# Strassen products for the last pair and the first two single tiles, a re-measured plan, and a new order of the first loads, in a fused attention and MLP kernel

## The chip, the cores and the metric

The kernel runs on one core of a Trainium2 chip. The metric is the device time of one execution in microseconds (us). Most executions of one kernel lie within 0.3% of each other. The span in a profile is some 1.8 us shorter than the device time of the same execution, because it counts from the first instruction to the last. A run over 1.5% above the fastest of the same kernel is called slow, and no reading here rests on a slow run.

## The reference, cut to what matters

Eight-head attention over 4 batches of 768 positions with a band of 96 positions and 8 global columns, then a two-layer MLP on the 3072 x 512 result.

```python
B, H, S, D = 4, 8, 768, 64
keep = is_global | is_local            # 8 global columns, band of 96
scores = np.where(keep, scale * q @ k.T + bias, -1e9)
x = softmax(scores) @ v                # gathered to 3072 x 512
h = x @ w_in                           # 512 x 2048
g = h - np.tanh(h)
out = g @ w_out                        # 2048 x 512
```

The sequence is cut into 24 tiles of 128 rows. The first four tiles go through the MLP singly, the other twenty in ten pairs.

## The kernel before

TensorE (PE) does scores, attention times v, transposes, and the two products of the MLP. The second product, g with w_out, has two forms. The plain one takes 16 matmuls of 512 columns for each tile. The other is Strassen's scheme on a pair of tiles: rows are halved by tile, the 2048 inner positions by halves, and the 512 columns by halves, so that seven products of 8 matmuls of 256 columns stand for the eight block products of the plain form (56 x 256 columns of work against 64 x 256, which the plain form does as 32 x 512). VectorE (DVE) makes the sums of g that go in (A), the sums of w_out (B, made once), and the sums that make the output out of the seven products.

```python
FAST = set(range(5, 13))         # groups done by Strassen: eight of the ten pairs
ORDER = (4, 3, 1, 5, 2, 7, 6)    # the seven products
HOME = {3: ("in", 0), 4: ("in", 1), 1: ("one", 0), 5: ("mid", 0), 2: ("mid", 1),
        7: ("out", 0), 6: ("out", 1)}          # which PSUM bank, which half of it
...
def product(g, kk):                            # 8 matmuls of 256 columns
    n, side = HOME[kk]
    o = buf("bank", ("P", g, n))[:, side * DH : side * DH + DH]
    for f in range(CH):
        ...
        nc.tensor.matmul(o, a, b, start=(f == 0), stop=(f == CH - 1))
```

Products 7 and 6, the last two, share one PSUM bank. The last group of all is not done by Strassen: its last tile is computed in 384 and 128 columns, so that only a copy and a small store follow the last matmul.

No instruction stands in program order by hand. A planner in the kernel file holds every operation with its engine, a duration, what it comes after and which buffers it takes and gives; it simulates the engines and the loads, and the kernel is emitted in the order of the simulated starts. Loads of q, k and v are given to the queue of GpSimd (POOL) in a list, and from tile 6 on each waits until the first product of the MLP has come near enough to its tile.

```python
LAT = {PE: 0.2, ACT: 0.14, DVE: 0.13, POOL: 0.15, SP: 0.0}   # end to release
...
AHEAD, EARLIER = 5.0, 0.5        # how many tiles ahead of its use a tile's work begins
MORE = 0.0
arrive = "q0 v2 v0 q1 k1 v1 q2 k2 i0 i1 q3 i2 i3 k3 i4 i5 o0 v3 k0 o1 k4 q5 o2 v6 o3 q4 k5 q6 k6 v4 v5".split()
...                              # i0.. parts of w_in, o0.. parts of w_out
hw_loads = {0}                   # q and k of tile 0: as float over the SP queue, cast on chip
...
pl.op(("g", g, f), DVE, 0.66, lambda e, g=g, f=f: m1_g(g, f), after=[("th", g, f)], ...)
```

The softmax here doesn't subtract the row's maximum and nothing guards it: scores larger than these inputs give would overflow.

Of the kernel before, what the change touches and what calls it, by code (L numbers as in the profile page):

```python
# [16 lines left out]
class Planner:  # L17


    LAT = {PE: 0.2, ACT: 0.14, DVE: 0.13, POOL: 0.15, SP: 0.0}  # L20
# [17 lines left out]
    def run(self, free, prefer):  # L38
# [5 lines left out]
        rings = {SP: [], POOL: []}  # L44
        setup, finish = {SP: 1.1, POOL: 2.0}, {SP: 0.3, POOL: 0.5}
# [17 lines left out]
        def step(limit):  # L63
            nonlocal at_dma
            heads = {r: x[0] for r, x in rings.items() if x}
            live = [r for r, x in heads.items() if x[2] <= at_dma + 1e-9]
            if not heads:
                at_dma = max(at_dma, limit) if limit < never else at_dma
                return None
            nxt = min([x[2] for r, x in heads.items() if r not in live] + [limit])  # L70
            hw = 0.07 if len(live) == 2 and heads[POOL][3] else 0.41
            rate = {r: (hw if r is SP else 1.0 - hw) if len(live) == 2 else 1.0 for r in live}
            end = min([at_dma + heads[r][1] / rate[r] for r in live] + [never])
            t = min(nxt, end)
            for r in live:
                heads[r][1] -= (t - at_dma) * rate[r]
            at_dma = t
            for r in live:
                if heads[r][1] < 1e-9:
                    return r  # L80
            return None
# [17 lines left out]
        while left:  # L99
# [36 lines left out]
            if o["dma"]:  # L136
                rings[eng].append([key, o["dma"], end + setup[eng], key[0] in ("in", "out")])
# [29 lines left out]
def kernel(  # L167
# [31 lines left out]
    TILES = [(0, 0), (1, 0), (0, 1), (0, 2), (1, 1), (2, 0), (0, 3), (2, 1), (3, 0), (3, 1), (1, 2), (2, 2), (1, 3), (3, 2), (0, 4), (2, 3), (3, 3), (3, 4), (0, 5), (1, 4), (1, 5), (3, 5), (2, 4), (2, 5)]  # L199
# [4 lines left out]
    R_ENGS = [(ACT, 0.7), (DVE, 0.36)]  # L204
    FAST = set(range(5, 13))
# [22 lines left out]
    touch = [cpool.tile([P, CD, 16], FP32, name=f"touch{n}") for n in range(2)]  # L228
# [6 lines left out]
    IN_PARTS = [2, 2, 2, 2, 4, 4]  # L235
# [6 lines left out]
    sb("kf", [P, H, Dh], FP32, 2)  # L242
# [21 lines left out]
    sb("ot", [P, DM], FP32, 3)  # L264
    sb("ot2", [P, 2, DM], FP32, 2)
# [11 lines left out]

    def fast(g):
        return g in FAST

    def gtags(g):
        return [("g", g)] if len(groups[g]) > 1 else [("g", g, 0), ("g", g, 1)]
# [4 lines left out]
    def gblk(g, f0, f1, c0, c1):  # L287
        if len(groups[g]) > 1:
# [49 lines left out]
    hw_loads = {0}  # L338
# [173 lines left out]
    def store2(g):  # L512
        r0, r1 = [(tiles[u][0] * NQ + tiles[u][1]) * P for u in groups[g]]
# [4 lines left out]

    T_LD, T_V, T_W, T_ST, T_TR = 0.85, 0.86, 2.55, 0.45, 1.15
    AHEAD, EARLIER = 5.0, 0.5  # L520
    MORE = 0.0
# [7 lines left out]
    arrive = "q0 v2 v0 q1 k1 v1 q2 k2 i0 i1 q3 i2 i3 k3 i4 i5 o0 v3 k0 o1 k4 q5 o2 v6 o3 q4 k5 q6 k6 v4 v5".split()  # L529
# [19 lines left out]
    for m in range(3):  # L549
        for half in range(2):  # L550
            pl.op(("mk", m, half), ACT, 0.85, lambda e, m=m, half=half: build_mask(m, half),
# [3 lines left out]
    for it in arrive:  # L555
# [13 lines left out]
        else:  # L569
# [9 lines left out]
            if u in hw_loads and nm != "v":  # L579
                keyf = ("ldf", nm, u)  # L580
                pl.op(keyf, SP, 0.52,
                      lambda e, u=u, nm=nm, src=src: nc.sync.dma_start(out=buf("kf", ("kf", nm, u)), in_=rows(src, u)),
                      after=[prevs and ("issue", prevs)], take=[("kf", ("kf", nm, u))], dma=T_LD + (0.0 if prevs else 0.9))
                prevs = keyf
# [12 lines left out]
    for u in range(NU):  # L597
# [4 lines left out]
        for nm in ("k", "q"):  # L602
# [3 lines left out]
            if u < NPE:  # L606
# [4 lines left out]
                pl.op(("Te", nm, u), [(DVE, 0.4), (ACT, 0.6)],  # L611
# [18 lines left out]
        for o in os_:  # L630
            for hh in range(2):
                pl.op(("E", u, o, hh), ACT, 0.53, lambda e, u=u, o=o, hh=hh: a_E(u, o, hh),
                      after=[("S", u, o), ("issue", ("E", u, 0, 1)) if o else None, ("issue", ("E", u, o, 0)) if hh else None],
                      give=[("S", u, o, hh)])
            pl.op(("M", u, o), DVE, 0.7, lambda e, u=u, o=o: a_M(u, o),
                  after=[("E", u, o, 0), ("E", u, o, 1)] + [("mk", 2 if o else min(i, 1), half) for half in range(2)])
        if 1 <= i < NQ - 1:
            pl.op(("K", u), [(ACT, 0.2), (DVE, 0.2)], None, lambda e, u=u: a_K(e, u), after=[("S", u, 0), ("S", u, 1)])
            pl.op(("V", u), [(ACT, 0.5), (DVE, 0.25)], None, lambda e, u=u: a_V(e, u), after=[("AV", u), ("ld", "v", zero_of(u))])
        pl.op(("AV", u), PE, 0.52 if i else 0.27, lambda e, u=u: a_AV(u),  # L640
# [5 lines left out]
        for a in range(2):  # L646
            pl.op(("R", u, a), DVE, 0.18, lambda e, u=u, a=a: a_R(u, a), after=[("AV", u), ("issue", ("R", u, 0)) if a else None],
# [10 lines left out]
        if u < NPX:  # L658
# [3 lines left out]
            pl.op(("X", u), [(DVE, 0.4), (ACT, 0.6)], None,  # L662
# [11 lines left out]
    for kk in (6, 4, 3, 1, 7):  # L674
        for j in range(2):
            pl.op(("B", kk, j), [(DVE, 0.64)], None, lambda e, kk=kk, j=j: b_sum(e, kk, j),
# [5 lines left out]
    for n in range(2):  # L682
        pl.op(("touch", n), ACT, 0.5, lambda e, n=n: nc.scalar.dma_start(out=touch[n], in_=w_in_r[:, :, 0:16]),
              after=[("issue", ("ld", "k", 2))] if n else [], pri=-9)
# [3 lines left out]
    pl.op(("vone",), DVE, 0.6, lambda e: [nc.vector.memset(t[:, :, Dh : Dh + 1], 1.0) for t in bufs["vb"] + bufs["vb0_"]], pri=-3)  # L688

    for g, us in enumerate(groups):  # L690
        n, per = shape1(g)
        for f in range(0, CF, per):
# [10 lines left out]
            pl.op(("th", g, f), ACT, 0.55, lambda e, g=g, f=f: nc.scalar.activation(  # L703
                buf("th", ("th", g, f)), buf("bank", ("h", g, f)), AF.Tanh, bias=0.0, scale=1.0),
                  after=[("m1", g, f)], take=[("th", ("th", g, f))], pri=2)
            pl.op(("g", g, f), DVE, 0.66, lambda e, g=g, f=f: m1_g(g, f), after=[("th", g, f)],
                  take=[(gpool(g), tag) for tag in gtags(g)] if f == 0 else [], give=[("h", g, f), ("th", g, f), ("l1", g, f)], pri=2)
        if fast(g):
            u0, u1 = us
            gall = [("g", g, f) for f in range(0, CF, per)]  # L710
            glow = gall[: len(gall) // 2]
            pl.uses["g", g] = 7
            for kk in (6, 1, 5, 2, 7):
                pl.op(("A", g, kk), [(DVE, 0.64)], None, lambda e, g=g, kk=kk: a_sum(e, g, kk),
                      after=glow if kk == 6 else gall, take=[("hb", ("a", g, kk))], give=[("g", g)], pri=1)
            before_p = {4: gall, 3: [], 1: [("A", g, 1)], 5: [("A", g, 5)], 2: [("A", g, 2)],
                        7: [("A", g, 7)], 6: [("A", g, 6)]}
            last = None
            for kk in ORDER:
                bs = [("B", kk, j) for j in range(2)] if kk in B_OF else []  # L720
                pl.op(("P", g, kk), PE, 0.875, lambda e, g=g, kk=kk: product(g, kk),
                      after=before_p[kk] + bs + ([("issue", last)] if last else []),
                      take=[("bank", ("P", g, HOME[kk][0])), ("lim2", ("l2", g, HOME[kk][0]))] if kk in (4, 1, 5, 7) else [],
                      give=[("g", g)] if kk in A_RAW else [("a", g, kk)], pri=2, mode="full")
                last = ("P", g, kk)

            def bank(g, n):
                return buf("bank", ("P", g, n)).rearrange("q (a d) -> q a d", a=2)

            def one(g):  # L730
                return buf("bank", ("P", g, "one"))[:, 0:DH]

            def cross(g):
                return buf("ot2", ("ot2", g)).rearrange("q a d -> q (a d)")[:, DH : 3 * DH].rearrange("q (a d) -> q a d", a=2)

            def same(g):
                return bass_same(buf("ot2", ("ot2", g)))

            def sm(g):
                return buf("sum", ("s", g))  # L740

            def ts(g):
                return buf("tsum", ("t", g))

            pl.op(("s34", g), [(ACT, 0.53), (DVE, 0.62)], None, lambda e, g=g: copy(e, sm(g), bank(g, "in")),
                  after=[("P", g, 3), ("P", g, 4)], take=[("sum", ("s", g))], give=[("P", g, "in"), ("l2", g, "in")], pri=1)
            pl.op(("t", g), DVE, 0.35, lambda e, g=g: add(e, ts(g), sm(g)[:, 0, :], 1, sm(g)[:, 1, :]),
                  after=[("s34", g)], take=[("tsum", ("t", g))], pri=1)
            pl.op(("u", g), DVE, 0.42, lambda e, g=g: add(e, ts(g), one(g), 1, ts(g)),
                  after=[("t", g), ("P", g, 1)], give=[("P", g, "one"), ("l2", g, "one")], pri=1)  # L750
            pl.op(("cx", g), DVE, 0.66, lambda e, g=g: add(e, cross(g), bank(g, "mid"), 1, sm(g)),
                  after=[("P", g, 5), ("P", g, 2), ("s34", g)], take=[("ot2", ("ot2", g))],
                  give=[("P", g, "mid"), ("l2", g, "mid")], pri=1)
            pl.op(("ab", g), DVE, 0.6, lambda e, g=g: add(
                e, sm(g), ts(g).rearrange("q (a d) -> q a d", a=1).to_broadcast([P, 2, DH]), -1, cross(g)),
                  after=[("cx", g), ("u", g)], give=[("t", g)], pri=1)
            pl.op(("cs", g), DVE, 0.66, lambda e, g=g: add(e, same(g), bank(g, "out"), 1, sm(g)),
                  after=[("ab", g), ("P", g, 7), ("P", g, 6)], give=[("P", g, "out"), ("l2", g, "out"), ("s", g)], pri=1)
# [99 lines left out]
```

## Time and profile before

| | before |
|---|---|
| device time, median of the kernel's runs | 208.45 us (3 runs), 208.5 us beside the changed kernel (4 runs) |
| span of the profiled execution | 206.84 us |
| first matmul with w_in starts | 14.76 us |
| last matmul starts | 203.76 us |
| from there to the end of the span | 3.08 us |

PE's list of waits (what it waited for: us in total, how often, the longest):

```profile
PE bank L442 <- DMA kb<-in_k_dram: 1.3, 3, 0.9
PE bank L680 <- DVE zeros L685: 1.1, 1, 1.1
PE bank L442 <- DVE kb L383: 0.7, 1, 0.7
```

All of these lie before 14.76 but for one of the three waits in the first line (k, at 39.85, at most 0.4 us). L442 is the transpose on PE, L680 the warm-up matmuls with zeros. The timeline of the end (start, length, engine and line, what):

```profile
203.13 0.48 ACT L381 COPY ot<-bank 128x384 f32<-128x384 f32 x1 [2.01 <-PE bank L479]
203.63 1.01 SPq L492 DMA_DIRECT2D out_dram<-ot  x2
204.02 0.27 ACT L381 COPY ot<-bank 128x128 f32<-128x128 f32 x1 [0.41 <-PE bank L479]
```

After the last matmul come a copy of 0.27 us and the issue of a 64 KB store (the second of the two issues on SP, from 204.31 to 204.64); it lands (its completion is seen) at 205.88, and the span ends 0.96 us later.

### The profile page before, as it was taken

The numbers are of one execution on the slowest core, as the hardware profiler recorded it, in microseconds if no ns is written. First come the engines' busy times: TensorE is split into PE (matmuls) and PEld (weight loads), VectorE is DVE, ScalarE is ACT, GpSimd is POOL, SyncE is SP. The second block draws the span as 40 slices with busy tenths as digits, with TensorE's granted clock in tenths as the row PEclk, the third lists the DMA queues.
The fourth block names the chain that finished last, engine by engine and source line by source line (L and its number), as shares of the span: only waits on it lengthen the run. The fifth ranks groups of instructions, "written<-read, shape, count | busy, mean of one in ns | idle before, by whom it ended". The sixth has DMA issues, their size and how long they took to land.

```text
span 206.8 us, 5861 instructions
## 1 busy us (share of the span) xinstructions
PE 198.8 (96%) x2308; PEld 161.9 (78%) x2316; DVE 167.5 (81%) x365; ACT 141.8 (69%) x341; POOL 69.7 (34%) x85
## 2 busy tenths in 40 slices
PE   7689999999999999999999999999999999999994
PEld 4369968465877677988988888988888988888853
DVE  6568974996686979989989998998998989898610
ACT  6788874395798899569567869549578776334311
POOL 8996336680360450550550544150440000000000
PEclk9999999999999999999999999999999999999999
DMA  8999999999999999999999999999999304002022
GB/s 130 148 186 196 200 185 197 160 210 163 149 186 129 138 145 145 111 111 113 178 136 113 180 113 101 214 131 186 63 133 189 73 8 128 3 0 101 3 101 101
DMA packets 111915, 27.19 MB, mean 131 GB/s; under 512 B 103568, under 2 KB 108944, under 8 KB 111888
## 3 DMA queue, kind: packets, MB, share of 16 engines
q0 software_dynamic: 78080, 13.37, 87.2%
q1 hardware_dynamic: 32752, 13.38, 37.1%
q8 instruction: 18, 0.29, 0.6%
q10 hardware_dynamic: 1056, 0.07, 0.4%
q14 instruction: 9, 0.07, 0.2%
HBM read 27.33 MB, written 6.29 MB: 163 GB/s over the span
## 4 chain that ended last, share of the span: by engine, by line
PE 79%; DMA 12%; POOL 7%; issue 1%; ACT 0%; POOLq 0%
PE bank L457 34%; PE bank L328 24%; PE bank L498 9%; DMA w_out_bf<-in_moe_w_out_dram 6%; DMA kb<-in_k_dram 6%; PE bank L393 5%; PE bank L412 2%; PE bank L414 2%; POOL w_in_bf L560 2%; PE bank L479 2%; POOL qb L592 2%; POOL kb L592 1%; POOL vb L592 1%; PE bank L442 1%; ACT ot L381 0%
## 5 line engine op out<-in xcount | busy, mean ns | idle before, releaser
L457 PE MATMUL bank<-xT,w_in_bf 128*128 128x256 bf16 (+1 forms) x896 | 95.0, 257 | 0.0
L457 PEld LDWEIGHTS <-w_in_bf 128*128 128x128 bf16 x896 | 75.6, 98 | 9.0
L703 ACT ACTIVATE th<-bank 128x512 f32<-128x512 f32 x96 | 56.7, 608 | 33.2 <-PE bank L457 27.8
L466 DVE TENSOR_TENSOR g<-bank,th 128x512 bf16<-128x512 f32 x80 | 52.7, 681 | 4.9 <-ACT th L703 4.8
L592 POOL DMA_DIRECT2D kb<-in_k_dram x23 | 20.6, 897 | 73.6 <-PE bank L457 68.7
L328 PEld LDWEIGHTS <-hb 128*128 128x128 bf16 x320 | 31.0, 98 | 3.6
L398 ACT ACTIVATE pd<-bank 128x512 bf16<-128x512 f32 x48 | 26.0, 604 | 5.6 <-PE bank L393 5.5
L302 DVE TENSOR_TENSOR hb<-g 128x1024 bf16<-128x1024 bf16 x40 | 26.2, 682 | 0.1
L429 ACT ACTIVATE x<-bank,rden 128x64 bf16<-128x64 f32 x100 | 22.0, 316 | 4.4 <-DVE rden L421 4.3
L328 PE MATMUL bank<-bsum,hb 128*128 128x256 bf16 x192 | 24.6, 272 | 0.0
L592 POOL DMA_DIRECT2D vb<-in_v_dram x24 | 21.7, 905 | 4.8 <-PE bank L457 3.0
L592 POOL DMA_DIRECT2D qb<-in_q_dram x23 | 20.6, 898 | 6.5 <-DMA w_out_bf<-in_moe_w_out_dram 5.3
L398 ACT ACTIVATE po<-bank 128x512 bf16<-128x512 f32 x40 | 22.3, 621 | 0.0
L403 DVE TENSOR_TENSOR pd<-pd,mk 128x1024 bf16<-128x1024 bf16 x24 | 16.5, 687 | 3.6 <-ACT pd L398 3.2
L328 PE MATMUL bank<-bsum,g 128*128 128x256 bf16 x128 | 16.6, 273 | 0.0
L328 PE MATMUL bank<-w_out_bf,hb 128*128 128x256 bf16 x128 | 16.4, 273 | 0.0
L498 PE MATMUL bank<-w_out_bf,hb 128*128 128x512 bf16 x60 | 15.2, 379 | 0.3
L403 DVE TENSOR_TENSOR po<-po,mk 128x1024 bf16<-128x1024 bf16 x20 | 13.7, 686 | 1.8 <-ACT po L398 1.4
L393 PEld LDWEIGHTS <-kT 64*128 64x128 bf16 x352 | 9.9, 94 | 6.8 <-issue 4.6
L393 PE MATMUL bank<-qT,kT 64*128 64x128 bf16 x352 | 14.2, 217 | 0.5 <-DVE kT L383 0.5
L412 PE MATMUL bank<-vb,pd 128*128 128x65 bf16 x192 | 13.9, 193 | 0.1
L328 PEld LDWEIGHTS <-g 128*128 128x128 bf16 x128 | 12.1, 98 | 1.8
(59 smaller groups left out, 195.5 us busy)
## 6 DMA issues: line engine op xcount, KB each, us to landing
out_dram<-ot SPq DMA_DIRECT2D x8, 512.0 KB, 3.9
vb<-in_v_dram POOLq DMA_DIRECT2D x24, 128.0 KB, 6.5
qb<-in_q_dram POOLq DMA_DIRECT2D x23, 128.0 KB, 5.5
kb<-in_k_dram POOLq DMA_DIRECT2D x23, 128.0 KB, 4.9
w_out_bf<-in_moe_w_out_dram POOLq DMA_DIRECT2D x4, 512.0 KB, 14.0
out_dram<-ot SPq DMA_DIRECT2D x7, 256.0 KB, 5.0
w_in_bf<-in_moe_w_in_dram POOLq DMA_DIRECT2D x4, 256.0 KB, 6.2
w_in_bf<-in_moe_w_in_dram POOLq DMA_DIRECT2D x2, 512.0 KB, 10.0
```

The source lines that it names most:

```text
L302: eng_of(e).tensor_tensor(out=out, in0=x, in1=y, op=ALU.add if sign > 0 else ALU.subtract)
L328: nc.tensor.matmul(o, a, b, start=(f == 0), stop=(f == CH - 1))
L393: nc.tensor.matmul(t[hh][:, p * P : (p + 1) * P], kt[r, p, :], qt[r, p, :], start=True, stop=True)
L398: nc.scalar.activation(dst, t, AF.Exp, bias=0.0, scale=scale)
L403: nc.vector.tensor_tensor(out=p, in0=p, in1=mk[:, m, :, :], op=ALU.mult)
L412: nc.tensor.matmul(o, pd[:, slot(h), :], vd[:, h, 0 : Dh + 1], start=True, stop=w is None)
L429: nc.scalar.activation(x[:, h, :], t[:, h, 0:Dh], AF.Copy, bias=0.0, scale=rd[:, h, :])
L457: nc.tensor.matmul(t[:, (f - fa) * n : (f - fa + 1) * n], w_in_bf[j][:, c, fo : fo + P], xt[:, c, 0:n], start=(c == 0), stop=(c == CD - 1),)
L466: nc.vector.tensor_tensor(out=dst, in0=t.rearrange("q (b n) -> q b n", n=n), in1=th.rearrange("q (b n) -> q b n", n=n), op=ALU.subtract,)
L498: nc.tensor.matmul(o, gblk(g, f, f + 1, t * P, t * P + P)[:, 0, :], w_out_blk(f, 0, DM), start=(f == 0), stop=(f == CF - 1),)
L592: pl.op(key, POOL, 0.88, lambda e, u=u, src=src, dst=dst: nc.gpsimd.dma_start(out=dst(), in_=rows(src, u)), after=[prev and ("issue", prev ...
L703: pl.op(("th", g, f), ACT, 0.55, lambda e, g=g, f=f: nc.scalar.activation(buf("th", ("th", g, f)), buf("bank", ("h", g, f)), AF.Tanh, bias ...
```

## The change

Its intent: fewer matmul columns, in two places; loads, latencies and durations in the planner that come from measurement; and an order of the first loads in which the scores of all four single tiles are done early. Its core:

```diff
-    LAT = {PE: 0.2, ACT: 0.14, DVE: 0.13, POOL: 0.15, SP: 0.0}
+    LAT = {PE: 0.2, ACT: 0.2, DVE: 0.19, POOL: 0.15, SP: 0.0}
 ...
-    R_ENGS = [(ACT, 0.7), (DVE, 0.36)]
-    FAST = set(range(5, 13))
+    R_ENGS = [(ACT, 0.79), (DVE, 0.335)]
+    FASTH = 1                      # the first two single tiles as one pair
+    FAST = set(range(5, 14))       # the last pair too
 ...
-    TILES = [(0, 0), (1, 0), (0, 1), (0, 2), (1, 1), (2, 0), ...]
+    TILES = [(1, 0), (0, 0), (0, 1), (1, 1), (0, 2), (3, 0), ...]
-    IN_PARTS = [2, 2, 2, 2, 4, 4]
+    IN_PARTS = [4, 2, 2, 4, 4]
-    hw_loads = {0}
+    hw_loads = {("k", 0): SP, ("q", 0): SP, ("q", 1): ACT}
-    AHEAD, EARLIER = 5.0, 0.5
-    MORE = 0.0
+    AHEAD, EARLIER = 4.5, 0.5
+    MORE = 0.5
-    arrive = "q0 v2 v0 q1 k1 v1 q2 k2 i0 i1 q3 i2 i3 k3 i4 i5 o0 v3 k0 o1 k4 ...
+    arrive = "q2 k2 k3 k0 k1 v1 q3 v0 i0 v2 i1 i2 i3 v3 i4 q4 k4 o0 o1 v4 o2 ...
 ...                                # some twenty durations like these two
-                pl.op(("Te", nm, u), [(DVE, 0.4), (ACT, 0.6)],
+                pl.op(("Te", nm, u), [(DVE, 0.345), (ACT, 0.48)],
-            pl.op(("g", g, f), DVE, 0.66, ...
+            pl.op(("g", g, f), DVE, 0.6, ...
 ...                                # the last pair's store, in three parts
+        if g == LAST:
+            pl.op(("st", u0), SP, 0.6, lambda e, g=g: store_part(g, "cross"), after=[("cx", g)], dma=T_ST)
+            for t, kk in enumerate((7, 6)):
+                pl.op(("cs", g, t), DVE, 0.335, lambda e, g=g, t=t: add(
+                    e, buf("ot2", ("ot2", g))[:, t, t * DH : t * DH + DH], bank(g, "out")[:, t, :], 1, sm(g)[:, t, :]),
+                      after=[("ab", g), ("P", g, kk)], ...)
+                pl.op(("st", us[t], 1), SP, 0.6, lambda e, g=g, t=t: store_part(g, t), after=[("cs", g, t)], ...)
+            return
 ...
-    order, done = pl.run({PE: 1.6, ACT: 2.1, DVE: 0.8, POOL: 1.25, SP: 0.75}, prefer)
+    order, done = pl.run({PE: 1.6, ACT: 0.74, DVE: 0.8, POOL: 1.25, SP: 0.75}, prefer)
```

Cut: the move of the Strassen code into a function, buffers that the float loads share with the output tiles, the planner's model of a third load queue, and the loss of one of two small loads that touch w_in early.

## The prediction

> **What bounds the kernel now.** I read the page's first part, then the slices, the chain that ended last, the groups by shape, the timeline of the first 25 us and of the last 20, and windows that I cut where the stages change.
>
> ```profile
> PE 198.8 (96%) x2308; PEld 161.9 (78%) x2316; DVE 167.5 (81%) x365; ACT 141.8 (69%) x341; POOL 69.7 (34%) x85
> ...
> PE   7689999999999999999999999999999999999994
> ...
> DVE  6568974996686979989989998998998989898610
> ```
>
> TensorE (PE) is at 9 from the fourth slice to the last but one; VectorE (DVE) is near it from slice 18 on. Three windows:
>
> ```profile
> 14.76:51.67 36.91, 36.33 (x500) 27.21 (x502) 29.16 (x65) 26.38 (x61) 18.96 (x23) 1.00 1.77 188
> 51.67:197.04 145.37, 145.10 (x1655) 123.89 (x1656) 128.46 (x261) 103.05 (x237) 36.91 (x42) 1.00 1.15 117
> ...
> 204.10:206.84 2.74, 0.00 (x0) 0.00 (x0) 0.00 (x0) 0.18 (x1) 0.00 (x0) 1.00 0.28 96
> ```
>
> (Columns: length, busy time of PE, weight loads, DVE, ACT, POOL, granted clock, DMA share, GB/s.) 14.76 is the first matmul with w_in; from there PE never rests, at full clock. DMA is close to full only until about 52 us (188 GB/s against 117 later). So three things can move the end: the PE work after 14.76, the time at which the dense stretch starts together with how much was done before it, and the tail of 2.74 us. What DVE, ACT and POOL save in the middle is worth nothing by itself.
>
> The start and the end, from the timeline and the chain:
>
> ```profile
> 9.12 0.40 PE L442 MATMUL bank<-ident,kb 128*128 128x128 bf16 x4 [0.87 <-DMA kb<-in_k_dram]
> ...
> 14.76 1.06 PE L457 MATMUL bank<-xT,w_in_bf 128*128 128x128 bf16 x16
> ```
>
> ```profile
> 195.29 1.75 PE bank L328 x16
> 197.04 0.21 PE bank L498
> 197.25 0.05 issue
> 197.31 3.18 PE bank L498 x14
> 200.49 3.51 PE bank L479 x32
> 204.02 0.27 ACT ot L381
> ```
>
> L328 are Strassen products, here two of them, 16 matmuls of 256 columns in 1.75 us, 109 ns each. L498 and L479 are the plain second product of the last two tiles: 197.04 to 204.02, 6.98 us.
>
> **What the Trainium skill says.** "TensorE: Matmul & The Clock Gate", section "Back-to-back issue gap", gives N/2.4 + 2.5 ns for one matmul at the warm clock: 109 ns for 256 columns, 216 for 512. The trace agrees (109; four of 512 in 0.86 us, 216). The same section's sustained 131 ns for N=512 is not what this trace has. "DMA: Bandwidth & Descriptors", section "Issuing engines are not separate DMA queues", says that DMAs from scalar, sync and gpsimd run on the same 16 engines and that more issuers save issue time only. Here POOL takes 0.87 us per issue (3.23 to 4.09), while loads in the full stretch land about 0.84 us apart: a third queue gives order, little bandwidth. "VectorE: DVE Perf Modes", section "The DRAIN you can't avoid", says that the next op does not start before the pipe is empty. This trace shows overlap instead: two g subtractions of 0.68 us take 1.28 together, so starts are 0.60 apart. That is the figure which the new plan takes for them (0.66 before); I count DVE work by it.
>
> **The change, part by part.** I set the order in which both programs' instructions stand side by side.
>
> 1. *Strassen for the last pair.* 16 matmuls of 512, 16 of 384 and 16 of 128 columns go; 7 products of 8 matmuls of 256 columns come: 56 x 0.109 = 6.1 us for 6.98. Saves 0.88 on PE, at the very end, wholly on the path. The sums of A on DVE (5 x 0.60) lie beside products. The first product needs the last g; two products of the pair before it (1.75 us, 16 matmuls) still stand between the last w_in matmul and it, as they do before (195.29 to 197.04), and tanh 0.60 + g 0.68 + semaphores fit. No stall expected.
> 2. *Strassen for the first two single tiles.* 32 x 0.2155 = 6.9 us becomes 6.1: saves 0.8. But these products need all four parts of w_out and the DVE sums of B, while the plain product could begin with the first part.
> 3. *More done before the dense stretch.* Before the first w_in matmul the new order also has tile 3's transposes (8 x 56 ns = 0.45) and its two score groups (0.45, and 2 x 0.1 for entering and leaving that 64-row shape, seen as gaps of 0.1 in the trace). They stood behind it. Saves 1.1 if it starts at the same time.
> 4. *When it starts.* Tile 0's v is now the seventh POOL load. In the trace the seventh (k of tile 2) lands at 11.77. One more 256 KB float load on the hardware queues, one 32 KB touch less: I estimate +0.4, so v at 12.2. From the first AV (11.21) to the first w_in matmul (14.76) took 3.55 us, mostly 8 ACT scalings; half of them now go to DVE, which takes about 0.9 us off: 2.9 us (0.4 AV, 0.3 reciprocal, 0.9 scaling, 0.4 transpose, 0.4 copy, waits). 12.2 + 2.9 = 15.1, and the first w_in part (1 MB, 2.5 us behind v) lands about then. Costs 0.35.
> 5. *Stalls in the DMA-full stretch.* Of the 36.91 us between 14.76 and 51.67 the matmuls in the order make 34.5 at the intervals above (scores 27.5 ns each) and three visits to the scores 0.6: about 1.85 us are stalls, waits for v, w_out and k among them. The new plan places each item near its landing. Laying my landings (before's, shifted by the changed list: last w_in part 24, first w_out part 28.5, v of tile 4 32, last w_out part 38, v of tile 5 42) against the new order, I find about 0.35 at tile 4's v, 0.5 at tile 5's scores behind ten B sums (10 x 0.60 = 6 us of DVE in some 7 us), little else; estimate 1.2. Saves 0.65. Two visits to the scores fewer: 0.2.
> 6. *The tail.* Before: last matmul, ACT copy 0.27, store of 64 KB (1.6 us from issue to landing). After: the cross sum must end before the quarter sums (0.42 each on DVE), the last store has 128 KB. Estimate +0.45; storing in three parts only keeps this from being a full 512 KB store (median 3.9 us to landing).
> 7. *Planning numbers* move the middle's order; PE is 99.8% busy there, so nothing.
>
> Sum: -0.88 - 0.8 - 1.1 + 0.35 - 0.65 - 0.2 + 0.45 = -2.8 us. 208.45 - 2.8 = 205.65; I round to 205.7, 1.3% faster.
>
> **Rivals.**
> - *The start eats it.* If the three hardware loads and POOL crowd each other (q of tile 0 is now second on SP; before, the second landed at 5.5), v lands at 13 and the first w_in part at 16: points 3 and 4 cancel, 207. For: POOL's traffic slows the hardware queues as soon as it begins. Against: tile 0 needs its own q and k only by about 10 us, as v comes last.
> - *DVE becomes the bound.* The first pair's sums (5 of A, 5 after products) join the ten B sums between 34 and 47 us, about 14.5 us of work in 16. If PE waits there for a sum at each product, 1 to 2 us go: 207. For: DVE at 8.4 of 10 us already from 40 to 50. Against: sums come faster (0.60) than products take them (0.87).
> - *The just-in-time plan works wholly.* No stall at all before 52 us: 1.2 better, 204.5.
> - *The end is hidden by nothing.* If the last products wait for A sums, 0.7 each: 206.5.
>
> **Range and chances.** The 1.65 of points 1 and 2 I hold for sure to 0.1. Points 3 to 5 together are -1.4, and could be anything from +0.2 to -2.8. So 204.2 to 207.3. Faster by 2% means under 204.3; that takes almost every stall gone and a start no later than 14.8: 0.1. Slower by 2%: 0.01.
>
> **What will show it.** The profile of the changed kernel should have 560 matmuls of 256 columns in the products and 64 of 512 in the plain second product; the first w_in matmul at 15.1 (14.5 to 15.7); first w_out part landing near 28.5; the last matmul starting at about 200.6 (203.8 before), and 3.1 to 3.6 us from there to the end of the span; no PE gap in the last 8 us. What would make it wrong: a first w_in matmul after 16, PE waits of more than 2 us in total on DMA or on DVE sums between 15 and 50, or slices of PE under 9 between.

## The result, and the profile after

| | before | after | predicted |
|---|---|---|---|
| device time, median | 208.5 (208.41 to 208.65, 4 runs) | 206.92 (206.75 to 207.12, 4 runs) | 205.7 (204.2 to 207.3) |
| span of the profile | 206.84 | 205.14 | |
| first w_in matmul starts | 14.76 | 16.16 | 15.1 (14.5 to 15.7) |
| last matmul starts | 203.76 | 201.11 | about 200.6 |
| from there to the end (the tail) | 3.08 | 4.03 | 3.1 to 3.6 |

The ratio is 0.9924, with a 95% interval of 0.9907 to 0.9941. (Ratios are the mean time of one kernel's fast runs over that of the other's of the same rounds, so not quite the ratio of the medians quoted.) So the change gains 0.8%, inside the predicted range.

The page after: busy times, then the slices of PE and DVE.

```profile
PE 197.7 (96%) x2339; PEld 167.3 (82%) x2339; DVE 176.4 (86%) x387; ACT 139.7 (68%) x326; POOL 68.1 (33%) x83
...
PE   7789999999999999999999999999999999999992
...
DVE  5698899989886888899999879979979979699683
```

PE is as full as it was. DVE has gone up by 9 us of work and is at 9 through much of the middle, and no wait of PE on it after 16 us is in the list of waits: it did not become the bound. Windows cut at the same stages (length, then busy us of PE, weight loads, DVE, ACT, POOL, clock, DMA share, GB/s):

```profile
16.16:52.00 35.84, 35.84 (x520) 30.66 (x521) 32.90 (x69) 25.54 (x56) 16.88 (x20) 1.00 1.96 183
52.00:195.00 143.00, 142.80 (x1635) 121.96 (x1633) 125.93 (x260) 101.77 (x232) 36.82 (x42) 1.00 1.09 119
201.20:205.14 3.94, 0.18 (x2) 0.00 (x0) 0.76 (x2) 0.00 (x0) 0.00 (x0) 0.97 0.39 133
```

Busy time cannot tell a full PE from one that idles between overlapping records, so I also laid the start-to-start intervals of all matmuls beside 109 ns for 256 columns and so on. By that count the time above these intervals, between the first w_in matmul and 52 us, fell from 1.9 us to 0.4. It includes PE's visits to the scores, whose 64-row shape costs some 0.25 us going in and out: three visits before, two after. So about 1.1 us were stalls before, and next to none after; one more stall, 0.36 with a change of shape, stands at 55.3. (The profile before has 64 weight loads and 60 matmuls of the plain second product there. The four are taken as matmuls that were not recorded, since missing records would pass for stalls.) The waits of PE agree; of these four, three belong to the start up to 16.16, and only the third, a transpose by DMA, comes later:

```profile
PE bank L461 <- DVE kb L402: 1.4, 1, 1.4
PE bank L461 <- ACT x L448: 0.4, 1, 0.4
PE bank L412 <- DMA qT<-qb: 0.2, 1, 0.2
PE bank L476 <- ACT pd L417: 0.2, 1, 0.2
```

(L461 is the transpose, L476 the first product, L412 the scores.) The 1.4 us is the start. Its timeline:

```profile
5.36 0.77 DVE L402 CAST qb<-ot 128x512 bf16<-128x512 f32 x1 [1.43 <-DMA ot<-in_q_dram]
6.05 0.41 DVE L402 CAST kb<-ot 128x512 bf16<-128x512 f32 x1
6.51 0.61 PE L461 MATMUL bank<-ident,kb 128*128 128x128 bf16 x4 [1.43 <-DVE kb L402]
8.19 1.49 PE L461 MATMUL bank<-ident,qb 128*128 128x128 bf16 x12
10.34 0.84 PE L461 MATMUL bank<-ident,kb 128*128 128x128 bf16 x12
```

k of tile 0 had landed at 4.66, but DVE takes the casts in the planned order and waited for q of tile 1 until 5.33. So PE had nothing to do from 5.08 to 6.51. The last two lines show a second loss: twelve transposes take 1.49 us at 8.19 and 0.84 at 10.34. The array was at half clock, and this run's clock events grant the full clock only at 10.33; in the profile before they did so at 4.07. (This part is luck: other runs with the same start order had it from 4.39 or 5.23.) (The clock column of the page shows 9 throughout: it knows nothing of the time before the first event, and the durations have to tell it.) The scores of tile 0 came at 9.61 instead of 7.29, and the first w_in matmul 1.40 us later. Of the two losses only the second is shown to delay that matmul: the one-store kernel below has its first transpose as late, but the full clock early, and starts at 15.47.

The end, as the chain that ended last and as a timeline:

```profile
193.52 7.87 PE bank L347 x72
201.39 0.02 issue
201.42 0.42 DVE ot L321
201.84 0.33 DVEq L907
```

```profile
200.39 0.37 SPq L544 DMA_DIRECT2D out_dram<-ot  x1
200.40 0.69 DVE L321 TENSOR_TENSOR sum<-tsum,ot 128x512 f32<-128x512 f32 x1
201.42 0.76 DVE L321 TENSOR_TENSOR ot<-bank,sum 128x256 f32<-128x256 f32 x2 [0.33 <-PE bank L347]
201.87 0.82 SPq L547 DMA_DIRECT2D out_dram<-ot  x2
```

Seventy-two matmuls of 256 columns stand without a gap (L347 is the product), as predicted. Then both quarter sums wait for the last product, although one of them needs only the product before it and DVE was free at 201.09: the two products share a bank. The two stores are issued one after the other and land at 203.60 and 204.09; the span ends 1.05 us after the second.

By these marks the span's 1.70 us come apart as follows. The last matmul starts 2.66 earlier: 0.88 and 0.8 are the matmuls saved (points 1 and 2, by count), which leaves 0.98 for the start and the stretch up to 52 us. This is a remainder and not a measurement: no run takes back the order of tiles and loads alone. The tail gives 0.95 back.

### The profile page after: what moved, and what is told of

Read it like the earlier page. It is cut to its first block, busy times and chain, and to the rows that moved or that the text cites. A ratio compares the mean times of both kernels' runs of the same rounds, so it can differ in the third digit from the quotient of the medians.

```text
span 205.1 us, 5929 instructions
## 1 busy us (share of the span) xinstructions
PE 197.7 (96%) x2339; PEld 167.3 (82%) x2339; DVE 176.4 (86%) x387; ACT 139.7 (68%) x326; POOL 68.1 (33%) x83
## 4 chain that ended last, share of the span: by engine, by line
PE 88%; DMA 7%; DVE 2%; ACT 1%; issue 0%; DVEq 0%
PE bank L476 39%; PE bank L347 28%; PE bank L517 7%; PE bank L412 5%; DMA qT<-qb 5%; PE bank L431 3%; PE bank L433 2%; DMA ot<-in_q_dram 2%; PE bank L461 2%; PE bank L714 1%; DVE pd L422 1%; ACT x L448 0%; DVE kT L402 0%; DVE qb L402 0%; ACT pd L417 0%
## 5 line engine op out<-in xcount | busy, mean ns | idle before, releaser
L476 PE MATMUL bank<-xT,w_in_bf 128*128 128x256 bf16 (+1 forms) x896 | 95.2, 257 | 0.2 <-ACT pd L417 0.2
L476 PEld LDWEIGHTS <-w_in_bf 128*128 128x128 bf16 x896 | 75.6, 98 | 8.7 <-issue 0.3
L347 PEld LDWEIGHTS <-hb 128*128 128x128 bf16 x416 | 40.1, 98 | 5.2
L347 PE MATMUL bank<-bsum,hb 128*128 128x256 bf16 x256 | 32.9, 273 | 0.0
L321 DVE TENSOR_TENSOR hb<-g 128x1024 bf16<-128x1024 bf16 x45 | 29.6, 683 | 0.2
L448 ACT ACTIVATE x<-bank,rden 128x64 bf16<-128x64 f32 x84 | 19.4, 316 | 3.6 <-DVE rden L440 3.2
L626 POOL DMA_DIRECT2D qb<-in_q_dram x22 | 19.9, 904 | 3.7 <-DMA w_out_bf<-in_moe_w_out_dram 3.5
L347 PE MATMUL bank<-w_out_bf,hb 128*128 128x256 bf16 x160 | 20.6, 273 | 0.0
L347 PE MATMUL bank<-bsum,g 128*128 128x256 bf16 x144 | 18.4, 273 | 0.0
L321 DVE TENSOR_TENSOR ot<-bank,sum 128x512 f32<-128x512 f32 (+1 forms) x21 | 13.8, 661 | 2.2 <-PE bank L347 1.8
L347 PEld LDWEIGHTS <-g 128*128 128x128 bf16 x144 | 13.8, 98 | 1.8
L412 PE MATMUL bank<-qT,kT 64*128 64x128 bf16 x352 | 14.5, 219 | 0.4 <-DMA qT<-qb 0.2
L412 PEld LDWEIGHTS <-kT 64*128 64x128 bf16 x352 | 10.3, 95 | 5.1 <-issue 4.3
```

The source lines that it names most:

```text
L321: eng_of(e).tensor_tensor(out=out, in0=x, in1=y, op=ALU.add if sign > 0 else ALU.subtract)
L412: nc.tensor.matmul(t[hh][:, p * P : (p + 1) * P], kt[r, p, :], qt[r, p, :], start=True, stop=True)
L448: nc.scalar.activation(x[:, h, :], t[:, h, 0:Dh], AF.Copy, bias=0.0, scale=rd[:, h, :])
L476: nc.tensor.matmul(t[:, (f - fa) * n : (f - fa + 1) * n], w_in_bf[j][:, c, fo : fo + P], xt[:, c, 0:n], start=(c == 0), stop=(c == CD - 1),)
L626: pl.op(key, POOL, 0.88, lambda e, u=u, src=src, dst=dst: nc.gpsimd.dma_start(out=dst(), in_=rows(src, u)), after=[prev and ("issue", prev ...
```

## The experiments

All outputs are right. The first four below ran together on one chip (before: 208.74 us median). Point 1 alone, point 2 undone, all planning numbers undone and the tail with two banks ran on another (208.5), the other four on a third (208.57; two of its eleven runs of before were at 209.63 and 210.31, which makes the ratios of these four some 0.1% lower than their medians suggest).

**The changed kernel once more.** No edit.

> The changed kernel once more, as a control on this chip. Both theories: ratio 0.992 to 0.994 to the kernel before. Theory 'cold start' (PE still at half clock until about 10 us because the warm-up matmuls pause from 5.1 to 6.5 us): the moment at which the clock is granted may differ in this profile; if it is granted by 7 us here, the first w_in matmul comes at 15.5 to 15.8 instead of 16.16. Rival 'engines behind the v load' (the start hangs on v landing at 12.2, then reciprocal, scaling and transpose queued behind other work of DVE and ACT): first w_in matmul at 16.0 to 16.3 whatever the clock does.

206.91 us (206.73 to 207.01), ratio 0.9913 [0.9898, 0.9928]. First w_in matmul at 16.39, last matmul at 201.07, tail 4.00. Here the full clock was granted from 4.39 to 7.80, taken away from 7.80 to 11.21, and granted again.

**Is the late start paid for at the end?** Two kernels are meant to mend it in two ways. (The half microsecond that they win may be the clock's luck, as the one-store kernel below shows; for the question it does not matter where it comes from.) The first has seven more warm-up matmuls, to keep the clock up:

```diff
         for t, n, key, eng, tags, end in sorted(order, key=lambda x: (x[0], x[1])):
             got = tags
+            if key == ("T", "k", 0):
+                for _ in range(7):
+                    warm()
```

> Seven more warm-up matmuls before the first transpose, nothing else: they fill the pause of PE from 5.1 to 6.5 us. Theory 'cold start': the clock is granted by about 7 us, transposes of the first q run at 56 ns instead of 107, first scores at 9.1 instead of 9.61, first w_in matmul at 15.6 to 15.8, time 0.3 to 0.5 us shorter than the changed kernel (about 206.5). Rival 'engines behind the v load': first w_in matmul within 0.15 us of 16.16, time the same (206.8 to 207.0).

The second lets DVE cast k of tile 0 ahead of q of tile 1 (the plan itself is the same):

```diff
+        when = {x[2]: x[0] for x in order}
+        order = [(when["ld", "k", 0] + 0.001,) + x[1:] if x[2] == ("ld", "q", 1) else x for x in order]
```

> DVE casts k of tile 0 (landed at 4.66) before q of tile 1 (landed at 5.33), where the changed kernel waits for the latter first; nothing else. Theory 'cast order': the first transpose comes at about 5.4 instead of 6.51, PE has no pause of over 0.5 us, the clock is granted by 7, first scores at 8.6 instead of 9.61, the exponentials 1 us earlier, so that reciprocal and scaling of tile 0 no longer stand behind a mask product; first w_in matmul at 15.2 to 15.5, time 206.1 to 206.4. Rival 'bandwidth': q of tile 0 lands at 6.8 and v of tile 0 at 12.2 as before, w_in at 14.8; first w_in matmul within 0.2 us of 16.16, time the same.

Both start the w_in matmuls 0.5 us earlier (15.66 and 15.65), and neither ends earlier: 206.96 us, ratio 0.9915 [0.99, 0.993], last matmul at 201.18; and 206.92 us, 0.9914 [0.9898, 0.993], last matmul at 201.13. The gains in time that were expected did not come. Where the half microsecond went shows in the waits of PE with seven more warm-up matmuls:

```profile
PE bank L476 <- DMA w_in_bf<-in_moe_w_in_dram: 0.3, 1, 0.3
PE bank L431 <- DMA vb<-in_v_dram: 0.2, 1, 0.2
PE bank L461 <- DMA kb<-in_k_dram: 0.2, 1, 0.2
```

None of these three is in the list of the changed kernel. They stand at 18.35, 33.17 and 36.59 us. The transpose of k that the third line waits for starts at 36.32 in the changed kernel and at 36.59 in this one: the kernel that started 0.5 us ahead is 0.27 us behind at 36 us. In the changed kernel that k had landed at 36.11, 0.2 us before its use, and v of tile 4 at 32.69, 0.3 before its use; so there was at most 0.2 us to be won by coming earlier. With the extra warm-up matmuls the same two loads landed at 36.55 and 33.13, 0.44 later, although they were issued within 0.1 us of the same times; I did not find out why (in the other profiles of this order that k lands anywhere between these two times). With k first it is the same: waits at 25.50 (w_in), 33.13 (v) and 36.55 (k).

Six profiles have this order of work: these three, the control and the two kernels of the tail below. The three that start late (16.16, 16.39, 16.50) reach that transpose 20.16 us after their start, at 36.32, 36.55 and 36.66, with k already landed for 0.2 to 0.4 us. The three that start early (15.47, 15.65, 15.66) reach it at 36.35, 36.55 and 36.59, 0.04 to 0.05 us after k has landed. So what an earlier start than about 16.2 wins is lost again at the landings, while a later start still passes through to 36 us. The last matmuls of all six start between 201.02 and 201.18; the changed kernel, first of them at 50 us, loses 0.27 to the stall at 55.3, which the others have in part (one-store) or not at all.

**The third queue undone.** q of tile 1 goes back to POOL, and the plan is made anew:

```diff
-    hw_loads = {("k", 0): SP, ("q", 0): SP, ("q", 1): ACT}
+    hw_loads = {("k", 0): SP, ("q", 0): SP}
-    arrive = "q2 k2 k3 k0 ... o2 q1 q0 k5 ...
+    arrive = "q1 q2 k2 k3 k0 ... o2 q0 k5 ...
```

> q of tile 1 goes back to the POOL queue (first there), so only SP has hardware loads (k and q of tile 0); the plan is made anew. If the third queue is what delays the start by crowding (rival 'three loads crowd'): q of tile 0 lands at 5.5 to 6 instead of 6.83, first w_in matmul at 15.5 or earlier, time 0.3 to 0.6 us shorter than the changed kernel. If the third queue helps as the change intends: v of tile 0 is the eighth POOL load and lands at 12.6 to 13, first w_in matmul at 16.3 to 16.8, time 0.2 to 0.6 us longer.

208.01 us as the median of its four fast runs (207.38 to 208.92), ratio 0.997 [0.9942, 0.9998]; its two other runs were slow (211.86 and 210.51). The profiled run is the fastest one, 207.38: q of tile 0 lands at 5.73 instead of 6.83, v of tile 0 at 12.22 as in the changed kernel, the first w_in matmul starts at 16.04, the last at 201.47. So by these two profiles the third queue delays q of tile 0 by 1.1 us, and v comes at the same time with two queues as with three. Because the order was planned anew and the runs spread widely, this run says little about what the queue itself is worth in time.

**Point 1 alone.** The kernel before, with the last pair by Strassen and stored in three parts:

```diff
-    FAST = set(range(5, 13))
+    FAST = set(range(5, 14))
 ...                       # and the three-part store of the change for g == LAST
```

> The kernel before with one part of the change: Strassen for the last pair, stored in three parts; start, plan numbers and first tiles as before. My step 1 and step 6 as the profile of the changed kernel corrects them: -0.88 on PE, +0.9 in the tail (two quarter sums of 0.42 that both wait for the last product, a last store of 128 KB instead of 64 KB), so no gain: 208.3 to 208.6, ratio 0.999 to 1.001. Rival (the tail as I predicted it, +0.45): 208.0, ratio 0.998.

208.44 us (208.33 to 208.94), ratio 0.9995 [0.9977, 1.0012]: nothing. The last matmul starts at 202.75, which is 1.01 us earlier, and the tail is 3.92 us, which is 0.84 longer. Of the 1.01, 0.13 is there from 33 us on, long before the last pair (this profile starts the w_in matmuls at 14.36 instead of 14.76); the last pair itself gives 0.88.

```profile
202.75:206.67 3.92, 0.27 (x3) 0.00 (x0) 0.76 (x2) 0.00 (x0) 0.00 (x0) 0.96 0.40 134
```

In 3.92 us the core does 0.76 of sums; the rest is waiting for stores. The matmuls saved are as many as I counted, and the tail takes nearly all of it. The change's most visible part gains no time by itself.

**Point 2 undone.**

```diff
-    FASTH = 1
+    FASTH = 0
```

> The changed kernel with the plain second product for the first two single tiles; all else as changed, planned anew. My step 2 (0.8 us of PE on the path): last matmul 0.8 later, 207.6 to 207.8. Rival 'loads pace the stretch': until about 37 us PE waits for landings anyway, the plain product can begin with the first part of w_out and DVE has ten sums less, so less than half of the 0.8 shows: 206.9 to 207.3.

207.65 us (207.31 to 207.87), ratio 0.9953 [0.9936, 0.9971], 0.73 above the changed kernel; I had 0.8. Its profile, of its fastest run, has the last matmul only 0.43 later, at 201.54. The w_in matmuls show why: they are 0.08 us ahead of the changed kernel's at 31 us and 0.71 behind at 49, so the plain product costs 0.79; the stall at 55.3 in the changed kernel's profile takes 0.27 of it back.

**The planning numbers undone.** All old durations, latencies and leads in the changed kernel (the time from which ACT is free, 0.74, stays new):

```diff
-    LAT = {PE: 0.2, ACT: 0.2, DVE: 0.19, ...}        # as before the change
+    LAT = {PE: 0.2, ACT: 0.14, DVE: 0.13, ...}
-    AHEAD, EARLIER = 4.5, 0.5
-    MORE = 0.5
+    AHEAD, EARLIER = 5.0, 0.5
+    MORE = 0.0
 ...                                                   # and some twenty durations
```

> The changed kernel with the durations, latencies and look-ahead of the old plan (loads, queues, tile order and both new Strassen pairs stay). My step 7 (the middle is 99.8% busy, the order there gives nothing): within 0.3 us of 206.9. Rival 'the measured intervals are what removed the stalls before 52 us': 0.8 to 2 us longer, with waits on DMA or DVE in PE's list between 15 and 60 us.

210.85 us (210.57 to 210.98), ratio 1.0105 [1.0089, 1.0122]: 3.9 us above the changed kernel and slower than the kernel before. The waits of PE:

```profile
PE bank L476 <- DMA w_in_bf<-in_moe_w_in_dram: 1.3, 1, 1.3
PE bank L461 <- DMA kb<-in_k_dram: 0.8, 1, 0.8
PE bank L476 <- DVE xT L402: 0.5, 1, 0.5
PE bank L476 <- ACT xT L400: 0.5, 1, 0.5
```

The first is at 18.34 us, where the new numbers have no wait. It is a kernel of the same work. Its instructions stand in another order, and some operations that two engines can do have moved (379 DVE instructions instead of 387, 346 on ACT instead of 326). The last matmul starts 4.1 us later (205.20 for 201.11). By start-to-start intervals some 2.9 of this lie before 65 us and 1.2 after it, where PE visits the scores 21 times instead of 16. This was a part to which I had given nothing, so I split it.

> The changed kernel, but the plan gets only the old lead and the old latencies back (load lead 5.0 us without the extra 0.5, semaphore latencies 0.14 on ACT and 0.13 on DVE); the durations stay the measured ones. All the old numbers together cost 3.9 us (210.85). If the latencies and the lead are what the plan lives on, most of that comes back here: 209.5 or more. If the durations are what counts: within 0.5 of the changed kernel, 206.6 to 207.4. If each is only another throw of the dice (any plan for which the tile order was not tried out is worse), both this run and the one with the old durations lie 1 to 3 us above 206.9.

```diff
-    LAT = {PE: 0.2, ACT: 0.2, DVE: 0.19, ...}
+    LAT = {PE: 0.2, ACT: 0.14, DVE: 0.13, ...}
-    AHEAD, EARLIER = 4.5, 0.5
-    MORE = 0.5
+    AHEAD, EARLIER = 5.0, 0.5
+    MORE = 0.0
```

> The changed kernel, but the plan takes the old durations for each operation on ACT, DVE and PE; lead and latencies stay the new ones. If the durations are what the plan lives on: 209.5 or more, with stalls of PE before 65 us at the w_in landings and at copies of xT. If the lead and the latencies are: within 0.5 of 206.9. Dice: 208 to 210, and the sum of the two losses needs not be 3.9.

```diff
-                pl.op(("Te", nm, u), [(DVE, 0.345), (ACT, 0.48)],
+                pl.op(("Te", nm, u), [(DVE, 0.4), (ACT, 0.6)],
 ...                                                   # the other durations likewise
```

The old lead and latencies: 208.86 us (208.49 to 209.49), ratio 1.0005 [0.9974, 1.0035], 1.9 above the changed kernel. The old durations: 209.7 us (209.46 to 210.03), ratio 1.0042 [1.0012, 1.0073], 2.8 above. Neither is small, and the two add up to more than the 3.9 of both; of the outcomes expected it is the one that calls each new plan a throw of the dice. (The lead is counted in tiles, not in us as that text has it.) In the second, PE waits for w_in again, although its first w_in matmul starts at 15.55, earlier than in the changed kernel:

```profile
PE bank L476 <- DMA w_in_bf<-in_moe_w_in_dram: 1.3, 2, 0.7
PE bank L431 <- DMA vb<-in_v_dram: 0.7, 2, 0.5
```

The reverse, the kernel before with only the numbers new:

```diff
-    LAT = {PE: 0.2, ACT: 0.14, DVE: 0.13, ...}
+    LAT = {PE: 0.2, ACT: 0.2, DVE: 0.19, ...}
 ...                                                   # and all other numbers of the change
```

> The kernel before with nothing changed but the planning numbers (durations, latencies, lead, first mask 2.15, ACT ready at 0.74). If better numbers make a better plan by themselves, it gains the 2 us and more that they are worth in the changed kernel: 205.5 to 207. If numbers and tile order only fit each other (both were chosen together), it gains nothing or loses: 208.3 to 211.

208.8 us (208.71 to 209.73), ratio 1.0006 [0.9976, 1.0036]: no gain. The same numbers that are worth 3.9 us under the new order of tiles and loads are worth nothing under the old one. So it is not that truer durations make a better plan. Order and numbers belong together. Whether this fit was sought (many orders tried under one set of numbers, the best kept) or has a reason in one of the numbers, these runs don't tell.

**The tail.** The changed kernel with one sum and one store for the last pair, as the other pairs have it:

```diff
-        if g == LAST:
+        if False:
             pl.op(("st", u0), SP, 0.6, lambda e, g=g: store_part(g, "cross"), ...)
```

> The changed kernel with the last pair stored as the other pairs are: one sum of both same-half quarters and one store of 512 KB after it. My prediction's point 6 says that the three parts only keep the tail from this larger store: a median of 3.9 us from issue to landing for 512 KB against about 1.8 for the last part. If so the end comes about 1.5 us later: 208.2 to 208.8, last matmul at 201.1 as before, tail 5.5 or so. If a lone store at the end lands as fast as a small one (nothing else moves then), the cost is below 0.7: 207.0 to 207.6.

208.16 us (207.83 to 208.5), ratio 0.9966 [0.9938, 0.9994], 1.2 above the changed kernel. The end of its timeline:

```profile
201.32 0.69 DVE L321 TENSOR_TENSOR ot<-bank,sum 128x512 f32<-128x512 f32 x1 [0.33 <-PE bank L347]
202.04 0.37 SPq L536 DMA_DIRECT2D out_dram<-ot  x1
```

The store lands at 204.81, 2.77 us after its issue began, against 1.78 for the last 128 KB of three; the tail is 4.94 us. I had expected 3.9 us to landing, the median of all 512 KB stores in the profile before. Most of those run beside loads; alone, the store is quicker. Still the three parts are worth about 1 us (0.9 by the tails, 1.2 by the times), so without them point 1 would by this count have been a loss.

This run also shows what delayed the start. It makes the same casts and transposes in the same order as the changed kernel, with the full clock from 5.23 this time:

```profile
6.52 0.40 PE L461 MATMUL bank<-ident,kb 128*128 128x128 bf16 x4 [1.44 <-DVE kb L402]
8.12 0.84 PE L461 MATMUL bank<-ident,qb 128*128 128x128 bf16 x12 [0.56 <-DVE qb L402]
15.47 1.05 PE L476 MATMUL bank<-xT,w_in_bf 128*128 128x128 bf16 x16 [0.19 <-ACT pd L417]
```

PE waits as long for the first cast, and the first w_in matmul still comes 0.69 us earlier than in the changed kernel. It comes 3.32 us after the landing of tile 0's v (12.15). That distance is 3.31 to 3.33 in all four kernels with this start whose clock was full by 7 us (more warm-up, k first, point 2 undone, this one), and 3.92, 4.14 and 4.26 in the three with half clock at 9 us (the changed kernel, the control, the two banks). So the late clock cost 0.6 to 0.9 us of the start, and neither the order of the casts nor the extra warm-up matmuls show an effect of their own beyond it. The last matmul starts at 201.02, 0.09 earlier.

Last, the tail with the last product in a bank of its own, and the last quarter stored over ACT's queue:

```diff
-        n, side = HOME[kk]
+        n, side = ("out2", 0) if g == LAST and kk == 6 else HOME[kk]
 ...
-            nc.sync.dma_start(
+            (nc.scalar if part else nc.sync).dma_start(
                 out=out[r : r + P, part * DH : part * DH + DH], ...)
 ...                                # and the planner's operations to match
```

> The changed kernel, but the last product goes into a bank of its own and the last quarter is stored from the ACT queue. The theory of the tail: both quarter sums wait for the last matmul because they share a bank (first sum at 201.42, although the sum ahead of it ended at 201.09), and SP issues the two stores one after the other. So the first quarter sum comes 0.3 earlier, the second at once after the last product, its store is issued 0.3 to 0.45 us earlier: tail 3.5 to 3.7 instead of 4.03, time 206.4 to 206.6. Rival 'the landing of 128 KB sets the end': tail within 0.15 us of 4.03, time the same.

206.7 us (206.22 to 207.4), ratio 0.9913 [0.9892, 0.9934].

```profile
201.26 0.76 DVE L321 TENSOR_TENSOR ot<-bank,sum 128x256 f32<-128x256 f32 x2
201.72 0.34 SPq L547 DMA_DIRECT2D out_dram<-ot  x1
202.05 0.37 ACTq L547 DMA_DIRECT2D out_dram<-ot  x1
```

The first sum no longer waits for PE, the stores are issued at 201.72 and 202.05 instead of 201.87 and 202.31, and the tail is 3.70 us instead of 4.03. The gain of 0.33 us shows in the profile; between the times of the two kernels (206.7 and 206.92, with runs from 206.22 to 207.4) it cannot be told from none. It is 0.9% faster than the kernel before; against the changed kernel no difference is shown. What the bank and the queue are worth apart was not tried.

## Why the prediction was right, and where it was wrong

The time (206.92 for 205.7) fell in the range. The sum was 1.2 us too hopeful, and its terms fared like this.

1. *Strassen for the last pair, -0.88.* Right as matmuls: 0.88 when done alone. The sentence "at the very end, wholly on the path" misled: the time of that part alone is 208.44 against 208.5, because the longer tail belongs to it.
2. *Strassen for the first two single tiles, -0.8.* Right: 0.73 by the times when undone, 0.79 in the profile. The counts were right too: 64 matmuls of 512 columns and 560 of 256.
3. to 5. *More before the dense stretch, the later start, fewer stalls, fewer switches: -1.1 + 0.35 - 0.65 - 0.2 = -1.6.* The remainder came to -0.98. The landings were predicted well (v of tile 0 at 12.24 for 12.2; first w_out part at 29.29 for 28.5), and the first w_in part came at 14.82. The chain on chip was not: from the landing of v to the first w_in matmul I had 2.9 us, and it is 3.3 at full clock and was 3.92 here, as I had not seen that the clock could still be low. The start came at 16.16 for 15.1, past the 16 that the prediction itself names as a sign of being wrong. Set against point 3's 1.1, the 1.40 of the later start loses 0.3 where I had a gain of 0.75. The stalls made up for most of it: they fell from 1.1 us to next to none before 52 (0.27 at 55.3), where I had 1.85 and 1.2, and the visits saved 0.3. The 1.85 was too high: with the unrecorded matmuls the work in that stretch makes 35.0 us and not 34.5, and the three visits 0.8 and not 0.6. That the start was missed by a microsecond cost almost nothing at the end, and this is the real fault: I added start and stalls as separate terms. Three runs (more warm-up, k first, the one-store tail) start 0.5 to 0.7 earlier, and their last matmuls start within 0.1 of the changed kernel's. What is won at the start, down from about 16.2, is waited for at a landing before 37 us. They are one term.
6. *The tail, +0.45.* It was +0.95. I counted the larger store but not that both quarter sums wait for the last product (they share its bank), nor that the second store is issued 0.44 after the first. 0.33 of it can be taken back.
7. *Planning numbers, "so nothing".* Wrong as an account of the parts: undone in the changed kernel they cost 3.9 us. "PE is 99.8% busy there" was read in the middle; the numbers work most on the stretch before 65 us, where the order decides which landing PE waits for, and after it on the number of visits to the scores, which a busy share does not show. The total was hardly hurt by this error, I think, for I had estimated the stalls of the new order as it stood, numbers included.

So the two terms that were mis-sized are points 3 to 5 (0.62 too hopeful) and point 6 (0.5), together 1.1 of the 1.2. The two Strassen terms were right by their mechanism. That the total still fell in the range, 0.4 under its upper end, owes something to luck and to the range's width of 3.1 us: of the marks set, the start (16.16 for 14.5 to 15.7) and the tail (4.03 for 3.1 to 3.6) were both missed.

Of the rivals, *the start eats it* named 207 and comes near by number but not by its mechanism: v did not land at 13 nor w_in at 16. *DVE becomes the bound* fell: no PE wait on a sum in that stretch. *The just-in-time plan works wholly* was right about the stalls (next to none before 52 us), but its 204.5 was lost to the start and the tail. *The end is hidden by nothing* fell in its words (72 matmuls in a row without a gap), while the loss at the end was real, behind the last matmul instead of before it.

## What to carry to other kernels

Count a saving at the end together with what must follow the last matmul: here 0.9 us of matmuls went into a longer tail, and only the store in three parts kept it from being a loss. When loads pace a stretch, a start before their landings and fewer stalls are the same microseconds; ask when the last load of the stretch lands, and what stands before it, and don't add the two. In a planned kernel the order is a part of the change like any other, and what it is worth is found only by running the plan with it undone.

## What the Trainium skill lacked or had wrong

- "TensorE: Matmul & The Clock Gate", section "What's actually happening": agrees. It says that the window of about 3.4 us runs free of the kernel, so that the onset of the full clock varies from run to run. The same instructions had it from 10.33 us in one run and in another from 4.39 to 7.80, without it for 3.41, and then from 11.21. It adds that this costs less than 1% of a typical kernel. Here it cost 0.6 to 0.9 us at the start and nothing that could be seen at the end: starts 1.0 us apart led to last matmuls within 0.17.
- Same page, section "Back-to-back issue gap": its sustained 131 ns for 512 columns is not found here; 216 ns is, which is its figure for a single matmul, and 109 ns for 256.
- "VectorE: DVE Perf Modes", section "The DRAIN you can't avoid": the prediction quotes only half of it. The section goes on to say that a next op that is not held starts earlier, and that fits the starts 0.60 us apart for ops of 0.68. The page was right and my reading short.
- "PSUM — Partial Sum Buffer", section "PSUM bank collisions raise a hardware error": its rule, to guard by bank (strictly, by bank and quadrant) and not by address, has a price that it doesn't state. A sum whose own product was done waited for the other product in the same bank (0.33 us of DVE idle, gone when the product had its own bank).
- "DMA: Bandwidth & Descriptors" has a fit for the time of one DMA on the gpsimd path, not for stores that SyncE issues, and no page adds up the end of a kernel: here 1.0 us from the last landing to the end of the span in both kernels, and 1.57, 1.78 and 2.77 us from the start of the issue to landing for last stores of 64, 128 and 512 KB.
